# A pacing constant for weight conversions: STEP2 from 2800 to 1900 in an attention and gated-FFN kernel

## The chip, the cores and the metric

The kernel runs on one core of one Trainium2 chip. The metric is the device time of one execution in microseconds (us). The core's engines are named as in the profile: PE does the matrix products and PEld loads their weights, DVE is the vector engine, ACT the scalar engine, POOL the general engine, and SP issues nearly all DMAs, in the order of its own queue. Each engine works its instructions off in a fixed order, which is settled when the kernel is built.

## The reference

Block-causal attention over 8 batches of 8 heads (576 positions, head size 64), and behind it a bilinear feed-forward layer over all 4608 tokens (512 to 1536 to 512), in float32:

```python
scores = scale * np.matmul(q, k.transpose(0, 1, 3, 2))
scores = np.where(mask, scores, -1000000000.0)          # by blocks of 64
attn = np.exp(scores - max); attn = attn / (sum + 1e-09)
x = (attn @ v).transpose(0, 2, 1, 3).reshape(B * S, H * D)
a = x @ w_a
b = x @ w_b
out = (a * b) @ w_out
```

The weights come in as 64-bit floats and are turned into float32 on the chip.

## The kernel before, in words

The hidden size of 1536 is 12 blocks of 128 ("f" 0 to 11), done in three passes of four blocks. A product in float32 is made of three products of rounded parts (high by high, low by high, high by low), so each operand is held as a high and a low part. The first pass runs beside the attention. The second and third pass each go over 6 pairs of token tiles of 384 (`tt`, 768 tokens each, here called a tile pair), and what follows is about these two passes alone.

For one tile pair and one f the function `pair_unit` (a unit) makes the products by a scheme with 7 products of 6 matmuls in place of 8: four into four PSUM banks y, x, w, v, and then a second one on top of x, w and v. Between them DVE must read the banks: L729 reads x (and a copy of y by ACT) and must be done before the second product on x, L731 reads w before the second on w, L733 reads v before the second on v. L735 to L739 make the two hidden tiles, ACT (L110) rounds each to its high part, and POOL (L113) makes its low part. After four units `pair_out` multiplies with W_out: 96 matmuls into 8 banks (L757), each of which DVE adds to a partial sum that SP loaded (L816), and SP stores the sum (L817).

Beside this, DVE and ACT prepare the next tile pair's x: SP loads four tiles of it (L665), `sums_x` forms differences (L675, L676, L679, L682) and low parts (L689 to L692).

The weights are converted by a generator, `convert_w`, that is advanced step by step. A part of W_a and W_b (two for each f) takes 6 steps: L139, L143, L145, L147 and L149 on DVE take the 64-bit numbers apart and build float32, L172 (four small ones) forms sums, L177 and L178 the low parts. A part of W_out (one for each f) takes 5 steps: L139 to L149 and one L113 on DVE. The parts for the third pass are converted during the second: each is loaded by SP (L124), written to memory when it is done (L205), and read back when the third pass's buffers come free (L842 for W_a and W_b, during the last tile pair, L857 for W_out, behind it). They are 8 x 6 + 4 x 5 = 68 steps in all.

How fast the generator is advanced is set by `background`: `k` counts matmuls of the units (4 x 42 = 168 for a tile pair), and after each one the generator is brought up to `start + k * T2 / 2.4 / pace` steps. From the end of the second pass's first tile pair on, `pace` is STEP2. What is left behind the last tile pair is done there in one go:

```python
if ps_ == 0 and tt == 0:
    background(1e4)
    conv = convert_w(parts(range(F1 + F2, NF)), nc.vector, paced=True, stage=stage)
    n_conv, start, k, pace = 0, 0, 0, STEP2
pair_out(fs, hs, nm, out)
if ps_ == 0 and tt == NT2 - 1:
    background(1e4)
```

A conversion's DVE instructions are bound to stand behind the latest L739 (`behind_of`, key "hf"). For the rest a scheduler in the kernel library settles each engine's order when the kernel is built, from the order of the code, its dependences and its own estimates of durations.

Of the kernel before, what the change touches and what calls it, by code (L numbers as in the profile page):

```python
# [38 lines left out]
MORE = 6  # L39
PREF = True  # L40
STEP = 800
STEP2 = 2800
LATE = 1
LO2 = lambda nc: nc.vector
CONVP = [1]*12
# [7 lines left out]
def attention_then_bilinear_ffn(  # L53
# [101 lines left out]
    def parts(fs):  # L155
        return [(f, i) for f in fs for i in range(KP)] + [(f, KP) for f in fs]
# [23 lines left out]
    def convert_w(todo, lo_eng, paced=False, stage=None):  # L180

        def ahead(f, i):
            return fetch(wab[f, :, i] if i < KP else wo[f], f"w{f}_{i}")

        raw = ahead(*todo[0])
        for k, (f, i) in enumerate(todo):
            now, raw = raw, ahead(*todo[k + 1]) if k + 1 < len(todo) else None
            xf, spare = yield from convert(now, f"w{f}_{i}", paced)
            if stage:
                st = stage.tile([P, 2, NW if i < KP else NO, P], F32R, tag="st", name=f"st{f}_{i}")  # L190
            if i == KP:
                if not stage and w_sb[f][1] is None:
                    new_wo(f)
                o = st.rearrange("p j c n -> p j (c n)") if stage else w_sb[f][1]
                split(o[:, 0], o[:, 1], xf, nc.scalar, lo_eng)
            elif f < F1:
                ab = w_sb[f][0]
                hi, lo = (ab[:, j, i].rearrange("p c n -> p (c n)") for j in range(2))
                split(hi, lo, xf, nc.scalar, lo_eng)
            else:  # L200
                ab = st if stage else w_sb[f][0][:, i]
                yield from sums(ab[:, 0], ab[:, 1], xf, spare, paced)
            if stage:
                f -= F1 + F2
                nc.sync.dma_start(wod[f] if i == KP else wabd[f, i], f32(st).rearrange("p j c n -> p (j c n)"))  # L205
            yield
# [536 lines left out]
    def pair_out(fs, hs, nm, out):  # L743

        todo = [(j, o) for j in (1, 0) for o in range(NO)]
        n = {}

        def run(j, o, fs_):
            k = j, o
            if k not in n:  # L750
                n[k] = 0, bank(f"pso{j}_{o}_{nm}")[:, :T2]
            i, ps = n[k]
            osl = slice(o * P, (o + 1) * P)
            for f in fs_:
                (hh, hl), wt = hs[f][j], w_sb[f][1]
                for a, b in ((0, hh), (0, hl), (1, hh)):
                    nc.tensor.matmul(ps, wt[:, a, osl], b, start=i == 0, stop=i == 3 * len(fs) - 1)  # L757
                    i += 1
            n[k] = i, ps
            if i == 3 * len(fs):  # L760
                out(j, o, ps)

        for k in todo[:2]:
            run(*k, fs[:-1])
        for k in todo[:2]:
            run(*k, fs[-1:])
        for k in todo[2:]:
            run(*k, fs)
# [34 lines left out]
    for ps_ in range(2):  # L803
        fs = list(range(F1 + ps_ * F2, F1 + (ps_ + 1) * F2))
        for tt in range(NT2):
# [42 lines left out]
# [5 lines that stand above are left out]
# [44 lines left out]
```

## Time and profile before

| | |
|---|---|
| time, three runs | 1268.36, 1269.23, 1271.0 us; median 1269.23 |
| the profiled execution | 1273.54 us, of which its span (first to last instruction) is 1271.6 |
| busy share of the span | PE 97%, PEld 92%, DVE 79%, ACT 54%, POOL 44% |
| second pass, units and products | about 697 to 983 us from the span's start |
| third pass | about 983 us to the end |
| DVE busy, 742 to 960 us | 189.30 of 218.00 us (87%) |
| DVE busy, 1000 to 1272 us | 173.84 of 272.00 us (64%) |
| PE busy, 960 to 1000 us | 35.45 of 40.00 us |

Times inside the execution are us from the span's start. In a timeline a row is: start, duration, engine, line, operation, tile written from tiles read, count, and in brackets the idle time of the engine before it and what ended it; short idle times have no bracket. In a table of stretches the columns are: the stretch, its length, busy time and count of PE, PEld, DVE, ACT and POOL, the clock that PE was granted (1.00 is full), the share of the DMA engines that was busy, and GB/s. A matmul's duration in the rows overlaps the next one's: 6 matmuls of 384 columns take 1.06 us.

### The profile page before, as it was taken

Reading aid. Unit: us, or ns where it says so; the run is one execution under the profiler, and the core shown is the slowest. Engines: PE = TensorE matmul, PEld = TensorE weight load, DVE = VectorE, ACT = ScalarE, POOL = GpSimd, SP = SyncE. Lnnn points to the kernel's source line nnn. Section 1 sums busy time; section 2 is a strip of 40 time slices with the busy share of each in tenths; the row PEclk is TensorE's granted clock in tenths of the full one; section 3 lists DMA queues with packets and bytes.
Section 4 is the critical chain, followed back from the end, with each engine's and each line's share of the span. In section 5 each row is a group of like instructions: output and inputs, shape, how many; then the busy total and the mean of one; then the engine's idle time right before and its main releaser. Section 6 shows DMA issues by size and latency. Waiting matters only on the chain.

```text
span 1271.6 us, 23516 instructions
## 1 busy us (share of the span) xinstructions
PE 1235.8 (97%) x7849; PEld 1172.4 (92%) x7849; DVE 1006.1 (79%) x2389; ACT 683.3 (54%) x1722; POOL 556.9 (44%) x679
## 2 busy tenths in 40 slices
PE   9988999999999999999998999999999999999998
PEld 5668999999999999999998999999999899999998
DVE  6979877777887777877799999899879877577553
ACT  5788787878887788777745423323313322122210
POOL 4667566556565565665423223222222223123231
PEclk8999999999999999999998999999999899999999
DMA  5557767777667767676225264364287752243131
GB/s 197 147 162 198 193 166 182 184 169 180 173 164 185 170 175 174 164 179 162 88 95 161 96 195 132 109 195 155 86 286 260 240 149 83 67 149 103 48 100 62
DMA packets 93496, 196.58 MB, mean 155 GB/s; under 512 B 11968, under 2 KB 52928, under 8 KB 93376
## 3 DMA queue, kind: packets, MB, share of 16 engines
q1 hardware_dynamic: 88768, 185.64, 51.8%
q10 hardware_dynamic: 4608, 9.44, 2.0%
q8 instruction: 63, 1.03, 0.3%
q14 instruction: 57, 0.47, 0.1%
HBM read 96.47 MB, written 47.19 MB: 113 GB/s over the span
## 4 chain that ended last, share of the span: by engine, by line
PE 74%; DVE 14%; issue 3%; DMA 3%; ACT 3%; POOL 2%; SPq 0%; ACTq 0%; DVEq 0%; POOLq 0%
PE pso_z L757 14%; PE ps L217 12%; PE tp L468 7%; PE psx_z L711 7%; PE psw_z L711 6%; PE pso L217 5%; PE psv_z L711 5%; PE s L392 4%; PE av L517 3%; PE psy_z L711 3%; PE av L523 3%; PE sl L392 2%; DMA kp<-kT 2%; DVE sw L147 1%; DVE nm L398 1%
## 5 line engine op out<-in xcount | busy, mean ns | idle before, releaser
L113 POOL TENSOR_TENSOR h_z<-u_z,h_z 128x384 fp32r<-128x384 f32 x96 | 111.0, 1157 | 395.4 <-ACT h_z L110 370.2
L217 PE MATMUL ps<-xh,wab 128*128 128x288 f32 x1024 | 241.4, 303 | 1.2 <-ACT a L241 1.2
L445 POOL TENSOR_SCALAR e<-e,rc 128x512 f32<-128x512 f32 (+3 forms) x256 | 153.1, 610 | 125.3 <-DVE rc L442 118.6
L757 PE MATMUL pso_z<-h_z,wo 128*128 128x384 f32 x1152 | 203.4, 335 | 1.2 <-POOL h_z L113 1.2
L757 PEld LDWEIGHTS pso_z<-h_z,wo 128*128 128x128 f32 x1152 | 199.7, 188 | 2.6 <-POOL h_z L113 2.6
L217 PEld LDWEIGHTS ps<-xh,wab 128*128 128x128 f32 x1024 | 171.9, 188 | 4.7 <-ACT a L241 1.4
L472 DVE TENSOR_TENSOR al<-tp,ah 128x512 fp32r<-128x512 f32 x224 | 131.5, 608 | 34.0 <-ACT ah L470 33.8
L217 PE MATMUL ps<-xl,wab 128*128 128x288 f32 x512 | 153.9, 301 | 0.0
L468 PE MATMUL tp<-ident,e 128*128 128x128 f32 x832 | 135.8, 278 | 11.1 <-POOL e L445 4.0
L470 ACT CAST ah<-tp 128x512 fp32r<-128x512 f32 x224 | 116.6, 533 | 50.8 <-PE tp L468 47.9
L110 ACT CAST h_z<-u_z 128x384 fp32r<-128x384 f32 x96 | 49.4, 514 | 164.4 <-DVE u_z L736 157.3
L217 PE MATMUL pso<-hh,wo 128*128 128x288 f32 x512 | 128.1, 311 | 4.4 <-ACT hh L110 4.4
L468 PEld LDWEIGHTS tp<-ident,e 128*128 128x128 f32 x832 | 100.4, 141 | 26.8 <-POOL e L445 10.4
L711 PE MATMUL psx_z<-xh,wab 128*128 128x384 f32 x384 | 118.2, 344 | 4.3 <-DVE u_z L729 3.6
L401 ACT ACTIVATE e<-s,nm 128x192 f32<-128x192 f32 (+2 forms) x192 | 101.7, 530 | 32.0 <-DVE nm L398 23.0
L711 PE MATMUL psw_z<-xh,wab 128*128 128x384 f32 x384 | 117.1, 341 | 1.3 <-DVE u_z L731 1.3
L711 PE MATMUL psv_z<-xh,wab 128*128 128x384 f32 x384 | 117.0, 339 | 0.0
L398 DVE TENSOR_REDUCE nm<-s 128x1 f32<-128x192 f32 (+3 forms) x256 | 109.9, 431 | 2.4
L217 PEld LDWEIGHTS ps<-xl,wab 128*128 128x128 f32 x512 | 96.4, 188 | 3.4
L217 PEld LDWEIGHTS pso<-hh,wo 128*128 128x128 f32 x512 | 88.4, 192 | 6.6 <-ACT hh L110 5.3
L113 POOL TENSOR_TENSOR v<-vr,v 128x320 fp32r<-128x320 f32 x56 | 50.4, 899 | 87.8 <-ACT v L110 71.3
L392 PE MATMUL s<-k,q 128*128 128x256 f32 x336 | 81.3, 322 | 3.1 <-ACT e L401 1.5
(142 smaller groups left out, 2926.3 us busy)
## 6 DMA issues: line engine op xcount, KB each, us to landing
k<-kp SPq DMA_DIRECT2D x112, 288.0 KB, 3.6
xr<-xd SPq DMA_DIRECT2D x48, 384.0 KB, 3.4
pt<-part SPq DMA_DIRECT2D x96, 192.0 KB, 3.5
q<-qp SPq DMA_DIRECT2D x112, 160.0 KB, 2.6
raww<-wab SPq DMA_DIRECT2D x24, 512.0 KB, 3.8
qp<-qT SPq DMA_DIRECT2D x32, 320.0 KB, 3.2
vr<-vm SPq DMA_DIRECT2D x64, 160.0 KB, 3.2
kp<-kT SPq DMA_DIRECT2D x32, 288.0 KB, 3.5
```

The costliest lines, as they stand in the source:

```text
L110: nc.scalar.copy(hi, src)
L113: return lo_eng.tensor_tensor(lo, src, f32(hi), op=ALU.subtract)
L217: mm = nc.tensor.matmul(ps, w_, d_, start=(i == 0), stop=(i == n - 1))
L392: mark = nc.tensor.matmul(ps[:, :w], qm[:, q0[t]:q0[t] + P], kk[:, :w], start=(i == 0), stop=(i == len(ks) - 1))
L398: nc.vector.tensor_reduce(nm[:, t:t + 1], view, axis=AX.X, op=ALU.max, negate=True)
L401: nc.scalar.activation(out, view, AF.Exp, bias=bias, accum_out=sm[:, t, :1])
L445: nc.gpsimd.tensor_scalar(ev, ev, rc[:, t:t + 1], 1.0, op0=ALU.mult, op1=ALU.mult)
L468: mark = nc.tensor.transpose(tp[:, c], src, ident)
L470: nc.scalar.copy(ah[:, :m, cols], tp[:, :m])
L472: return nc.vector.tensor_tensor(al[:, :m, cols], tp[:, :m], f32(ah[:, :m, cols]), op=ALU.subtract)
L711: nc.tensor.matmul(ps, wt[:, i, iw], j[:, ix], start=start and kp == 0 and i == 0 and j is xh, stop=kp == KP - 1 and i == 1, skip_group_ch ...
L757: nc.tensor.matmul(ps, wt[:, a, osl], b, start=i == 0, stop=i == 3 * len(fs) - 1)
```

## The change

One constant:

```diff
 STEP = 800
-STEP2 = 2800
+STEP2 = 1900
 LATE = 1
```

For a tile pair of 168 matmuls the generator is now advanced by 168 x 160 / 1900 = 14.1 steps in place of 168 x 160 / 2800 = 9.6. In the five tile pairs behind the first this comes to 70.7 in place of 48, so all 68 steps are made before the last `pair_out`, where 20 were left for the place behind it (all four parts of W_out). No instruction's work is changed: the same conversions stand in other places, and with them their DMAs.

In the rows that follow, `u_z_1_5` is the unit of tile pair 1 and f = 5, and `u_z_0_8` the first unit of the third pass; a row is a line, an operation, the tile written and the tiles read, and its size.

DVE in tile pair 1 of the second pass, between the units of f = 4 and f = 5, before:

```order
L739 TENSOR_TENSOR u_z_1_4_11090<-psx_z_1_4_11049,u_z_1_4_11090 128x384
L147 SCALAR_TENSOR_TENSOR sw_0_11057<-raww_0_11053,sw_0_11057 128x512
L149 TENSOR_TENSOR xw_0_11059<-mw_0_11058,sw_0_11057 128x512
L729 TENSOR_TENSOR u_z_1_5_11165<-psx_z_1_5_11133,u_z_1_5_11165 128x384
L172 TENSOR_TENSOR mw_0_11058<-xw_0_11059 128x128 x2
L172 TENSOR_TENSOR mw_0_11058<-mw_0_11058,xw_0_11059 128x128
L731 TENSOR_TENSOR u_z_1_5_11166<-psw_z_1_5_11134,u_z_1_5_11165 128x384
```

The same place now:

```order
L739 TENSOR_TENSOR u_z_1_4_11091<-psx_z_1_4_11049,u_z_1_4_11091 128x384
L149 TENSOR_TENSOR xw_0_11059<-mw_0_11058,sw_0_11057 128x512
L172 TENSOR_TENSOR mw_0_11058<-xw_0_11059 128x128 x2
L172 TENSOR_TENSOR mw_0_11058<-mw_0_11058,xw_0_11059 128x128
L177 TENSOR_TENSOR st_0_11144<-xw_0_11059,st_0_11144 128x384
L172 TENSOR_TENSOR mw_0_11058<-xw_0_11059,mw_0_11058 128x128
L729 TENSOR_TENSOR u_z_1_5_11176<-psx_z_1_5_11134,u_z_1_5_11176 128x384
L139 TENSOR_SCALAR sw_1_11189<-raww_1_11055 128x512
L178 TENSOR_TENSOR st_0_11144<-mw_0_11058,st_0_11144 128x512
L731 TENSOR_TENSOR u_z_1_5_11177<-psw_z_1_5_11135,u_z_1_5_11176 128x384
```

Six conversion instructions stand between the two units' work in place of two, and between L729 and L731 two large ones in place of three small ones.

DVE at the change of passes, ahead of the first L729 of the third pass, before (`raww_2` and `st_2` belong to parts of W_out, `xr_1` and `xt_1` to the x of the third pass's second tile pair):

```order
L149 TENSOR_TENSOR xw_2_13404<-mw_2_13403,sw_2_13402 128x512
L675 TENSOR_TENSOR xt_1_0_13682<-xr_1_13533,xr_1_13531 128x384
L139 TENSOR_SCALAR sw_2_13417<-raww_2_13400 128x512
L113 TENSOR_TENSOR st_2_13411<-xw_2_13404,st_2_13411 128x512
L816 TENSOR_TENSOR pt_3_5_0_13308<-pso_3_z_5_13385,pt_3_5_0_13308 128x384
L143 TENSOR_SCALAR mw_2_13418<-raww_2_13400 128x512
L147 SCALAR_TENSOR_TENSOR sw_2_13417<-raww_2_13400,sw_2_13417 128x512
L145 SCALAR_TENSOR_TENSOR mw_2_13418<-raww_2_13400,mw_2_13418 128x512
L676 TENSOR_TENSOR xr_1_13531<-xr_1_13531 128x384
L149 TENSOR_TENSOR xw_2_13419<-mw_2_13418,sw_2_13417 128x512
L729 TENSOR_TENSOR u_z_0_8_13498<-psx_z_0_8_13467,u_z_0_8_13498 128x384
```

The same place now:

```order
L675 TENSOR_TENSOR xt_1_0_13682<-xr_1_13533,xr_1_13531 128x384
L676 TENSOR_TENSOR xr_1_13531<-xr_1_13531 128x384
L816 TENSOR_TENSOR pt_1_5_0_13155<-pso_1_z_5_13413,pt_1_5_0_13155 128x384
L679 TENSOR_TENSOR xt_1_0_13682<-xr_1_13533,xr_1_13531 128x384
L682 TENSOR_TENSOR xt_1_0_13682<-xr_1_13533,xt_1_0_13682 128x384
L816 TENSOR_TENSOR pt_2_5_0_13359<-pso_2_z_5_13428,pt_2_5_0_13359 128x384
L816 TENSOR_TENSOR pt_3_5_0_13366<-pso_3_z_5_13443,pt_3_5_0_13366 128x384
L675 TENSOR_TENSOR xt_1_1_13762<-xr_1_13537,xr_1_13535 128x384
L676 TENSOR_TENSOR xr_1_13535<-xr_1_13535 128x384
L679 TENSOR_TENSOR xt_1_1_13762<-xr_1_13537,xr_1_13535 128x384
L682 TENSOR_TENSOR xt_1_1_13762<-xr_1_13537,xt_1_1_13762 128x384
L729 TENSOR_TENSOR u_z_0_8_13498<-psx_z_0_8_13467,u_z_0_8_13498 128x384
```

The conversions are gone from there, and all eight instructions on the next tile pair's x, which read all four loads `xr_1`, now stand ahead of L729; before, six of them came behind it.

SP's queue at the same place now, where those loads are issued:

```order
L665 DMA xr_1_13533<-xd 128x768
L812 DMA pt_3_5_0_13366<-part_58 128x384
L817 DMA part_59<-pt_2_5_0_13149 128x384
L817 DMA part_59<-pt_3_5_0_13151 128x384
L817 DMA part_59<-pt_0_5_0_13153 128x384
L665 DMA xr_1_13535<-xd 128x768
L817 DMA part_59<-pt_1_5_0_13155 128x384
L665 DMA xr_1_13537<-xd 128x768
```

The loads' places are nearly those of before (there `pt_1_5` was stored ahead of the third load, and three DMAs of the conversions stood between the third and the fourth). The fourth load is queued behind the store of `pt_1_5`, whose L816 now stands on DVE behind the first two instructions on `xr_1`.

## The prediction

> **What bounds the kernel now.** I read the table of stretches first, cut from one block of W_out products to the next, so that each row is one tile pair: three of the second pass, then its last one together with the first of the third pass, then two undisturbed ones of the third pass.
>
> ```profile
> 775.84:823.07 47.23, 47.01 (x265) 45.87 (x265) 42.77 (x71) 14.99 (x27) 13.27 (x10) 1.00 0.45 151
> 823.07:870.61 47.54, 47.21 (x265) 45.97 (x265) 43.01 (x71) 14.27 (x26) 12.95 (x10) 1.00 0.45 142
> 870.61:918.10 47.49, 47.15 (x266) 45.97 (x265) 41.25 (x65) 13.96 (x25) 13.27 (x10) 1.00 0.46 150
> 918.10:1019.16 101.06, 96.47 (x530) 94.86 (x529) 85.67 (x144) 30.99 (x54) 26.87 (x20) 0.97 0.72 247
> 1019.16:1065.64 46.48, 46.48 (x266) 46.32 (x265) 31.36 (x51) 11.38 (x21) 13.18 (x10) 1.00 0.34 103
> 1065.64:1112.09 46.45, 46.45 (x265) 46.28 (x265) 31.36 (x51) 11.38 (x21) 13.18 (x10) 1.00 0.33 102
> ```
>
> PE is busy throughout, and a tile pair on which nothing is converted takes 46.45 us. So PE's own work is the floor, and all that the change can move is what stands above it: 0.78, 1.09 and 1.04 us in tile pairs 2 to 4, and 101.06 - 2 x 46.45 = 8.2 us in the double stretch. With some 0.9 for tile pair 1 (an estimate after the other three) that is **12 us** in all. PE's longer waits and the clock show where the 8.2 went:
>
> ```profile
> 963.75 0.44 PE L711 MATMUL psx_z<-xh,wab 128*128 128x384 f32 x1 [1.15 <-DVE u_z L729]
> ...
> 969.85 0.62 PE L757 MATMUL pso_z<-h_z,wo 128*128 128x384 f32 x2 [0.41 <-POOL h_z L113]
> ```
>
> ```profile
> 989.82 0.44 PE L711 MATMUL psx_z<-xh,wab 128*128 128x384 f32 x1 [1.73 <-DVE u_z L729]
> 992.38 0.69 PE L711 MATMUL psw_z<-xh,wab 128*128 128x384 f32 x1 [1.25 <-DVE u_z L731]
> ```
>
> ```profile
> 990.00:1000.00 10.00, 8.75 (x34) 8.43 (x35) 8.05 (x17) 3.69 (x6) 1.41 (x1) 0.66 0.87 285
> ```
>
> About 2.1 belong to tile pair 5 (1.15 and 0.41, some 0.3 each for restarting and for an earlier short wait). The other **6.1 are the change of passes**: 1.73 and 1.25 of waiting, and about 3 of a clock granted at 0.66 over the ten us behind it. DVE's own rows there say whose work was in the way:
>
> ```profile
> 988.14 0.55 DVE L676 TENSOR_TENSOR xr<-xr 128x384 f32<-128x384 f32 x1
> 988.61 0.68 DVE L149 TENSOR_TENSOR xw<-mw,sw 128x512 f32<-128x512 f32 x1
> 989.21 0.55 DVE L729 TENSOR_TENSOR u_z<-psx_z,u_z 128x384 f32<-128x384 f32 x1
> 991.10 0.43 DVE L139 TENSOR_SCALAR sw<-raww 128x512 int32<-128x512 int32 x1 [1.34 <-DMA raww<-wo]
> ...
> 991.78 0.55 DVE L731 TENSOR_TENSOR u_z<-psw_z,u_z 128x384 f32<-128x384 f32 x1
> ```
>
> L729 is late behind conversions without a gap, and L731 behind a conversion that waits for its own load. Both go with the change. What comes in their place decides the sign.
>
> **What the change removes.** The 20 steps at the change of passes, and so the 6.1 us, if nothing else is late there. In tile pair 5 the last unit loses its conversions too.
>
> **What it adds in tile pairs 1 to 5.** The same DVE work, nearer together. The unit of DVE time that matters is the place between L739 and the next L729, where conversions are bound to stand. The view of DVE and of POOL at such a place of tile pair 3, which holds L149 and three of L172:
>
> ```profile
> 848.24 1.28 DVE L149 TENSOR_TENSOR xw<-mw,sw 128x512 f32<-128x512 f32 x1
> 849.55 1.20 DVE L172 TENSOR_TENSOR mw<-xw 128x128 f32<-128x128 f32 x2
> 850.67 0.28 DVE L172 TENSOR_TENSOR mw<-mw,xw 128x128 f32<-128x128 f32 x1
> 850.88 0.54 DVE L729 TENSOR_TENSOR u_z<-psx_z,u_z 128x384 f32<-128x384 f32 x1
> 851.35 0.28 DVE L172 TENSOR_TENSOR mw<-xw,mw 128x128 f32<-128x128 f32 x1
> 851.54 0.55 DVE L177 TENSOR_TENSOR st<-xw,st 128x384 fp32r<-128x384 f32 x1
> 852.01 0.55 DVE L731 TENSOR_TENSOR u_z<-psw_z,u_z 128x384 f32<-128x384 f32 x1
> ```
>
> ```profile
> 847.94 1.03 POOL L113 TENSOR_TENSOR h_z<-u_z,h_z 128x384 fp32r<-128x384 f32 x1 [17.00 <-ACT h_z L110]
> 849.31 1.09 POOL L113 TENSOR_TENSOR h_z<-u_z,h_z 128x384 fp32r<-128x384 f32 x1 [0.34 <-PE psx_z L711]
> ```
>
> Two of its DVE instructions each last until just after one of POOL's two L113 (848.97 and 850.40), which adds about 1.3 us whatever stands there. By the same conversions without POOL, at the change of passes, the rest is cheap:
>
> ```profile
> L113 DVE TENSOR_TENSOR st<-xw,st 128x512 fp32r<-128x512 f32 x4 | 2.8, 691 | 0.6 <-ACT st L110 0.6
> L147 DVE SCALAR_TENSOR_TENSOR sw<-raww,sw 128x512 int32<-128x512 int32 x4 | 2.8, 688 | 0.0
> ...
> L143 DVE TENSOR_SCALAR mw<-raww 128x512 int32<-128x512 int32 x4 | 1.7, 419 | 0.0
> ```
>
> Tile pairs 2 to 4 have three such places each, all of two or three large instructions or of this kind, for 0.78 to 1.09 us: **0.33 for a place**. So this length is just beyond what PE's first products cover, and each further instruction is paid at its distance from the next one's start: 0.6 for a large one, 0.35 for L139 or L143, 0.47 for L177 and 0.2 for an L172. [...] Were instead every conversion at such a place slowed as L149 is, by 0.6, the three long places below would be 1.2 dearer each, and the sum 3.6 higher.)
>
> The order of the changed kernel gives, unit by unit:
> - three long places (tile pairs 1, 2, 4) that end with L177 and the fourth L172 ahead of L729: 0.33 + 0.47 + 0.2 = 1.0, and behind L729 an L139 and an L178 ahead of L731: 1.0 where 0.66 (L172 and L177, above) just fitted, 0.3. Together 1.3 each;
> - three places with L143, L147 and L145, in tile pairs 2, 4 and 5: one more 0.47 than the usual, 0.8 each;
> - six usual places and two of L139 and L143, 0.33 each;
> - in tile pair 3 L177 and L172 ahead of an L731 (0.5), and three more pairs of L139 with L178 or L113 ahead of an L731 or L733, 0.3 each;
> - one L147 more at the end of tile pair 1. There DVE has no slack:
>
> ```profile
> 795.98 0.55 DVE L729 TENSOR_TENSOR u_z<-psx_z,u_z 128x384 f32<-128x384 f32 x1
> ```
>
> ```profile
> 796.58 0.44 PE L711 MATMUL psx_z<-xh,wab 128*128 128x384 f32 x1
> ```
>
> so another 0.6. The sum is 3.9 + 2.4 + 2.6 + 0.5 + 0.9 + 0.6 = 10.9, and with 0.3 for the next pair's L675 and L676 in tile pair 5 it is 11.2, against 0.9 + 2.9 + 2.1 = 5.9 before: **5.3 us more**. I would not trust it to better than 2.
>
> **What comes at the change of passes instead.** The unit's L729 now stands behind all eight instructions on `xr_1`, the last four of which need its third and fourth load. The rows for these loads (SP's issues, ACT's first reader, and the medians to landing of the two earlier, the two later, and the four of the third pass's first tile pair):
>
> ```profile
> 978.51 0.48 SPq L665 DMA_DIRECT2D xr<-xd  x1
> ...
> 989.09 0.92 SPq L665 DMA_DIRECT2D xr<-xd  x1
> ```
>
> ```profile
> 983.93 0.84 ACT L683 CAST xh<-xr 128x768 fp32r<-128x768 f32 x1 [1.53 <-DMA xr<-xd]
> ```
>
> ```profile
> xr<-xd SPq DMA_DIRECT2D x2, 384.0 KB, 4.5
> ```
>
> ```profile
> xr<-xd SPq DMA_DIRECT2D x2, 384.0 KB, 5.8
> ```
>
> ```profile
> xr<-xd SPq DMA_DIRECT2D x4, 384.0 KB, 3.4
> ```
>
> On the clock of before: nothing ahead of the second load is changed, so it is issued at 978.5 and there at 983.9. DVE, free since about 981.3, then does L675, L676 and the L816 of `pt_1_5` (3 x 0.5); SP stores that and only then issues the fourth load, at about 985.7. With 4.5 us to land it is there at 990.2; four instructions (1.9) and L729 (0.55) end at 992.7. PE ran dry at 989.82 - 1.73 = 988.1 before; ten W_out products that ran ahead in the stalls of tile pair 5 now come behind it, so it wants L729 at about 988.7. **PE waits 4.0 us**, and by 3.4 to 5.8 us of landing 2.9 to 5.3; if the second load too lands in 3.4, 2 less. The transfers of `raww` and `wod` that shared this stretch are gone, so I take 4.5 and not 5.8. Nothing else can run in the wait: in the changed order PE's next row is the second product on x of that unit.
>
> The clock: 1.73 and 1.25 idle within 4.3 us cost it half its rate for some 7 us. Less did not:
>
> ```profile
> 960.00:970.00 10.00, 8.44 (x47) 7.80 (x46) 8.87 (x18) 4.77 (x8) 2.29 (x3) 1.00 0.67 253
> ```
>
> 4.0 idle in one piece is more than either, so I count the same 3 us again. The change of passes then costs 4.0 + 0.1 + 3 = 7.1 in place of 6.1. **Sum**: +5.3 + 1.0 = +6.3. The profiled execution took 1273.54 us (2 around its span of 1271.6), 4.3 above the median of 1269.23; the same difference put on the median gives **1275.5 us**.
>
> **The rivals.**
> - *The wait without the clock's drop*: 3 less, 1272.5. [...] 0.18.
> - *The loads come in time*: if the fourth lands before about 986 on this clock, L729 is ready by 988.7 and the change of passes is free: 5.3 - 6.1 = -0.8, 1268.4. It would need the second load by 982 and the fourth in 2.5. 0.13.
> - *Faster*: the loads come in time, and the added steps in the tile pairs cost no more than those of before, 1.0 x 14.1 / 9.6 = 1.5 for each of five, 7.3 in place of 5.9: +1.4 - 6.1 = -4.7, **1264.5**. It is decided by the same landing at 986, and by the long places costing 0.5 and not 1.0. 0.09.
> - *The clock drops in the tile pairs too*: a long place puts 1.0 and 0.2 of idle within 2 us. Each drop would cost 3: 1278 to 1285. Tile pair 5 had 1.15 and 0.41 at a clock of 1.00 (above). 0.08.
>
> That the change might not do what it says is no rival: the order shows no conversion behind the last L816 of the second pass.
>
> **How the numbers follow.** The forecast has 0.52 and, by the landing, 1272 to 1279 as its own range. About 0.2% (2.5 us) is what a measurement of this kernel can tell from no change. Faster by more: the third rival and a little of the second, 0.10. Within it: most of the second, half of the first, 0.22. Slower: the rest, 0.68. The range of 1267.5 to 1280 leaves out the third rival, the low end of the second and most of the fourth.
>
> **What would show it.** Tile pairs 1 to 4 at 48 to 49.5 us from one block of W_out to the next, and the waits for L729 of 0.7 to 0.9 at the three long places; L675 on `xr_1` with an idle time of DVE that a load ends, twice; the first second product on x of the third pass behind a wait of 3 to 5 us, and a clock under 0.8 there. It would be wrong if the double stretch of tile pair 5 and the next is under 96 us, or if tile pairs 1 to 4 stay at 47.5.

## The result, and the profile after

| | before | changed |
|---|---|---|
| median of six runs | 1268.83 us | 1278.23 us |
| lowest to highest | 1263.68 to 1271.34 | 1277.07 to 1280.99 |
| the profiled execution, its span | 1273.54, 1271.6 | 1277.07, 1275.3 |

The ratio is 1.0062, with a 95% interval of 1.0041 to 1.0083: **slower, by some 7.9 us** by the ratio (the two medians differ by 9.4), where +6.3 was forecast. The median of 1278.23 us lies inside the stated range, 2.7 above the forecast of 1275.5.

The tables of stretches below are cut from the last W_out product of one tile pair to the last of the next: tile pairs 1 to 5 of the second pass, and as the sixth row the first tile pair of the third pass with the change of passes ahead of it. The columns are those of the prediction's tables. Before:

```profile
745.17:792.14 46.97, 46.67 (x265) 45.78 (x265) 41.66 (x68) 13.69 (x26) 13.22 (x10) 1.00 0.44 137
792.14:839.37 47.23, 47.01 (x265) 45.87 (x265) 42.77 (x69) 14.65 (x25) 12.98 (x10) 1.00 0.47 153
839.37:886.92 47.55, 47.22 (x265) 45.98 (x265) 42.98 (x72) 15.61 (x27) 13.26 (x10) 1.00 0.48 158
886.92:934.41 47.49, 47.15 (x266) 45.97 (x266) 40.56 (x65) 12.09 (x22) 13.26 (x10) 1.00 0.44 139
934.41:983.15 48.74, 47.13 (x265) 46.17 (x265) 40.17 (x67) 13.11 (x23) 13.24 (x10) 1.00 0.78 277
983.15:1035.63 52.48, 49.49 (x266) 48.69 (x266) 46.34 (x80) 19.03 (x31) 13.77 (x10) 0.93 0.67 218
```

The changed kernel:

```profile
742.52:791.08 48.56, 47.32 (x266) 45.93 (x265) 44.96 (x78) 16.07 (x29) 13.35 (x10) 1.00 0.49 153
791.08:840.55 49.47, 47.32 (x265) 45.67 (x265) 46.00 (x78) 16.31 (x28) 12.94 (x10) 1.00 0.53 181
840.55:889.23 48.68, 47.42 (x266) 45.88 (x266) 44.68 (x74) 14.56 (x27) 13.18 (x10) 1.00 0.49 162
889.23:937.92 48.69, 47.34 (x265) 45.76 (x265) 43.37 (x70) 14.70 (x26) 13.37 (x10) 1.00 0.50 162
937.92:985.71 47.79, 47.22 (x265) 45.91 (x265) 39.66 (x60) 13.64 (x23) 12.94 (x10) 1.00 0.76 264
985.71:1039.20 53.49, 47.93 (x265) 47.45 (x265) 35.41 (x59) 13.46 (x23) 13.14 (x10) 0.94 0.45 144
```

Row by row the change costs 1.59, 2.24, 1.13, 1.20, then -0.95, and +1.01 in the last: **5.2 us in tile pairs 1 to 5 and 1.0 at the change of passes, 6.2 in all.** In the last row DVE does 11 us less work than before (35.41 against 46.34) and PE still needs 1 us more: the work is gone and another wait stands in its place. PE's rows with the longer waits show both kinds:

```profile
755.30 0.44 PE L711 MATMUL psx_z<-xh,wab 128*128 128x384 f32 x1 [0.77 <-DVE u_z L729]
796.10 0.44 PE L711 MATMUL psx_z<-xh,wab 128*128 128x384 f32 x1 [0.44 <-DVE u_z L729]
803.92 0.44 PE L711 MATMUL psx_z<-xh,wab 128*128 128x384 f32 x1 [0.27 <-DVE u_z L729]
812.34 0.44 PE L711 MATMUL psx_z<-xh,wab 128*128 128x384 f32 x1 [0.72 <-DVE u_z L729]
820.79 0.45 PE L711 MATMUL psx_z<-xh,wab 128*128 128x384 f32 x1 [0.72 <-DVE u_z L729]
860.99 0.44 PE L711 MATMUL psx_z<-xh,wab 128*128 128x384 f32 x1 [0.63 <-DVE u_z L729]
870.53 0.44 PE L711 MATMUL psw_z<-xh,wab 128*128 128x384 f32 x1 [0.42 <-DVE u_z L731]
902.00 0.44 PE L711 MATMUL psx_z<-xh,wab 128*128 128x384 f32 x1 [0.78 <-DVE u_z L729]
910.05 0.44 PE L711 MATMUL psx_z<-xh,wab 128*128 128x384 f32 x1 [0.31 <-DVE u_z L729]
958.45 0.45 PE L711 MATMUL psx_z<-xh,wab 128*128 128x384 f32 x1 [0.38 <-DVE u_z L729]
995.85 0.69 PE L711 MATMUL psx_z<-xh,wab 128*128 128x384 f32 x1 [5.56 <-DVE u_z L729]
```

Each of the waits in the tile pairs costs its idle time and about 0.26 more until PE's matmuls keep step again: at 755.30 the matmul starts 1.11 us behind the one before it and the next 0.28 behind that, where 0.177 each is the rule. The three long places are those at 755.30, 812.34 and 902.00. The last row is the first second product on x of the third pass, 0.69 us long where the others take 0.44 or 0.45, at half the clock (0.50 granted from 992.27 to 999.10):

```profile
990.00:1000.00 10.00, 4.44 (x17) 4.15 (x16) 4.10 (x8) 0.00 (x0) 0.00 (x0) 0.66 0.98 358
```

Before, the same ten us had 0.66 too, with 34 matmuls where there are 17 now.

DVE's rows ahead of that wait, SP's issues, and the time to landing of the last of them:

```profile
984.88 0.56 DVE L675 TENSOR_TENSOR xt<-xr,xr 128x384 f32<-128x384 f32 x1 [2.05 <-DMA xr<-xd]
985.47 0.56 DVE L676 TENSOR_TENSOR xr<-xr 128x384 f32<-128x384 f32 x1
985.95 0.55 DVE L816 TENSOR_TENSOR pt<-pso_z,pt 128x384 f32<-128x384 f32 x1
...
992.99 0.56 DVE L675 TENSOR_TENSOR xt<-xr,xr 128x384 f32<-128x384 f32 x1 [4.50 <-DMA xr<-xd]
...
995.25 0.55 DVE L729 TENSOR_TENSOR u_z<-psx_z,u_z 128x384 f32<-128x384 f32 x1
```

```profile
986.53 0.32 SPq L817 DMA_DIRECT2D part<-pt  x1
986.95 0.37 SPq L665 DMA_DIRECT2D xr<-xd  x1
```

```profile
xr<-xd SPq DMA_DIRECT2D x1, 384.0 KB, 5.9
```

The chain of the prediction can be read off: L816 (985.95) ends, SP stores its tile (986.53), only then issues the fourth load (986.95). That takes 5.9 us to land, and DVE stands with L729 behind it.

### The profile page after: what moved, and what is told of

Same layout as the page of the kernel before. It is cut to its first block, busy times and chain, and to the rows that moved or that the text cites. A ratio compares the mean times of both kernels' runs of the same rounds, so it can differ in the third digit from the quotient of the medians.

```text
span 1275.3 us, 23521 instructions
## 1 busy us (share of the span) xinstructions
PE 1235.5 (97%) x7849; PEld 1170.6 (92%) x7849; DVE 1005.7 (79%) x2389; ACT 683.0 (54%) x1722; POOL 554.7 (43%) x679
## 3 DMA queue, kind: packets, MB, share of 16 engines
q8 instruction: 63, 1.03, 0.3%
## 4 chain that ended last, share of the span: by engine, by line
PE 69%; DVE 17%; DMA 4%; issue 4%; ACT 3%; POOL 2%; SPq 0%; ACTq 0%; DVEq 0%; POOLq 0%
PE pso_z L757 13%; PE ps L217 12%; PE tp L468 7%; PE psx_z L711 6%; PE psw_z L711 6%; PE pso L217 5%; PE psv_z L711 5%; PE s L392 4%; PE av L517 3%; PE av L523 3%; PE psy_z L711 2%; PE sl L392 2%; DMA kp<-kT 2%; DVE nm L398 1%; DVE sw L147 1%
## 5 line engine op out<-in xcount | busy, mean ns | idle before, releaser
L113 POOL TENSOR_TENSOR h_z<-u_z,h_z 128x384 fp32r<-128x384 f32 x96 | 109.9, 1146 | 402.8 <-ACT h_z L110 385.7
L757 PE MATMUL pso_z<-h_z,wo 128*128 128x384 f32 x1152 | 203.1, 335 | 0.7 <-POOL h_z L113 0.7
L757 PEld LDWEIGHTS pso_z<-h_z,wo 128*128 128x128 f32 x1152 | 199.9, 188 | 1.9 <-POOL h_z L113 1.9
L113 POOL TENSOR_TENSOR v<-vr,v 128x320 fp32r<-128x320 f32 x56 | 50.2, 896 | 88.8 <-ACT v L110 63.5
L711 PEld LDWEIGHTS psx_z<-xh,wab 128*128 128x128 f32 x384 | 71.5, 189 | 17.5 <-DVE u_z L729 17.5
```

Of the source, the lines that this page charges most:

```text
L113: return lo_eng.tensor_tensor(lo, src, f32(hi), op=ALU.subtract)
L711: nc.tensor.matmul(ps, wt[:, i, iw], j[:, ix], start=start and kp == 0 and i == 0 and j is xh, stop=kp == KP - 1 and i == 1, skip_group_ch ...
```

## The experiments

The stretches are cut as above. Where an edit adds two lines to the kernel, the line numbers behind them are two higher in its rows (L731 is L729 then, L735 is L733, L741 is L739, L759 is L757, L818 is L816, L691 to L694 are L689 to L692).

| stretch, us | tile pair 1 | 2 | 3 | 4 | 5 | first of pass 3 | sum |
|---|---|---|---|---|---|---|---|
| before | 46.97 | 47.23 | 47.55 | 47.49 | 48.74 | 52.48 | 290.5 |
| before, again | 46.99 | 47.23 | 47.49 | 47.44 | 48.73 | 51.15 | 289.0 |
| changed | 48.56 | 49.47 | 48.68 | 48.69 | 47.79 | 53.49 | 296.7 |
| changed, again | 48.54 | 50.07 | 48.64 | 48.73 | 47.83 | 54.70 | 298.5 |
| x behind the first unit | 48.53 | 49.94 | 48.64 | 48.65 | 47.83 | 46.47 | 290.1 |
| loads issued by ACT | 48.55 | 49.58 | 48.67 | 48.73 | 47.83 | 46.34 | 289.7 |
| conversions behind L733 | 46.42 | 53.29 | 46.32 | 46.66 | 46.32 | 54.04 | 293.1 |
| capped at 48 steps | 48.51 | 49.81 | 48.67 | 47.03 | 46.49 | 51.89 | 292.4 |
| both edits, 1900 | 46.39 | 53.63 | 46.32 | 46.64 | 46.32 | 46.47 | 285.8 |
| both edits, 2000 | 46.86 | 46.46 | 52.81 | 46.32 | 46.63 | 47.83 | 286.9 |
| both edits, 2200 | 46.32 | 46.32 | 46.32 | 46.32 | 46.92 | 47.40 | 279.6 |
| both edits, 2800 | 46.51 | 46.32 | 46.32 | 46.47 | 46.72 | 48.52 | 280.9 |

### Do the two profiles repeat?

The kernel before and the changed one, each profiled once more.

> The kernel before, unchanged, profiled a second time. The first profile has the second pass from 697.0 us and, from the last W_out product of its first tile pair to that of the third pass's first, 290.5 us. Theory (the stages from the second pass on repeat, and it is the first pass that differs from run to run): these stages at 290 to 291 again, each tile pair within 0.3, the start of the second pass anywhere from 691 to 700. Rival (the second pass itself differs from run to run, and the profile shown was a bad one): the stages 2 or more under 290.5.

> The changed kernel, unchanged, profiled a second time. The first profile has the second pass from 694.3 us and the same stages at 296.7 us, with a wait of 5.6 us for the third pass's first L729. Theory: stages at 296 to 297.5 again, the wait at 5 to 6, the start of the second pass anywhere from 692 to 700. Rival (the landing of the fourth load is chance): the wait falls to under 4 or rises over 7, with the stages by as much.

The tile pairs repeat within 0.1 us, but for tile pair 2 of the changed kernel (0.6, in the wait at 796.10, which was 1.04 the second time). The change of passes doesn't: 51.15 against 52.48, and 54.70 against 53.49. Neither theory had that: the waits are nearly the same (1.75 and 0.89 the second time before, 5.33 in the changed kernel), but the half clock covers other work. In the changed kernel's first profile it lasted from 992.27 to 999.10, so 3.3 us of it fell on work behind the wait; in the second from 997.90 to 1004.73, and 5.9 did. The second profile's row:

```profile
988.91:1043.61 54.70, 49.37 (x266) 48.88 (x265) 35.30 (x59) 13.45 (x23) 13.13 (x10) 0.94 0.43 145
```

By the two pairs of profiles these stages cost +6.2 and +9.5; the runs say +7.9.

### Is the wait at the change of passes DVE's order alone?

The first edit binds the third pass's second x behind the last L739 of that pass's first unit:

```diff
             if nm == f"0_{NT2}":
                 behind_of(ins, "hf")
+            if nm == "1_1":
+                behind_of(ins, "first")
...
                     background(start + k * T2 / 2.4 / pace)
+                if i == 0 and ps_ == 1 and tt == 0:
+                    last["first"] = last["hf"]
```

> The change, with one dependence more: the eight DVE instructions (first two of each half, the rest follow them) on the x of the third pass's second tile pair may only stand behind the last L739 of the third pass's first unit, not ahead of its first L729. Conversions stand where the change has them. Theory: the wait of 5.6 us for that L729 and the half clock behind it are only DVE's queue standing behind the late fourth load, so both go: 7 us less than the changed kernel, 1271 us (1269.5 to 1272.5), ratio to the kernel before 1.000 to 1.003; the granted clock is 1.00 from 985 on, and the double stretch of tile pair 5 and the next takes 94 to 95 us; tile pairs 2 to 4 stay at 48.7 to 49.2. Rival A, a wait takes its place (the x is late for the next tile pair, or L731 and L733 of the second unit stand behind the loads): 1274 to 1278. Rival B, most of the change's cost is in the tile pairs, and the wait was mostly paid before too: 1274 or more, with the clock unchanged.

The stretch of the change of passes falls from 53.49 to 46.47, which is the floor, and the clock is full:

```profile
941.68:989.52 47.84, 47.19 (x266) 45.93 (x266) 39.96 (x60) 13.63 (x23) 12.97 (x10) 1.00 0.76 264
989.52:1035.98 46.46, 46.46 (x265) 46.29 (x265) 35.51 (x58) 13.55 (x23) 13.54 (x10) 1.00 0.50 165
```

So all of the 7 us was DVE's queue standing behind a load that nothing needed yet. The total is 1273.59 us, a ratio of 1.0028 (1.0011 to 1.0045), 1.1 us above the range that I had given. The stages came out as said, but for tile pair 2 (49.94, where 49.2 was the top). The second pass began at 697.6 us in this profile and at 694.3 in the changed kernel's; more on this start below.

The second edit leaves DVE's instructions free and lets ACT issue the same four loads:

```diff
+    third = [False]
...
-            nc.sync.dma_start(
+            (nc.scalar if tt == 1 and third[0] else nc.sync).dma_start(
...
+                    third[0] = ps_ == 1
                     raw = load_x((tt + 1) % NT2)
```

> The change, with the four loads of the x of the third pass's second tile pair issued by ACT's queue in place of SP's, so that the fourth is no longer behind the store of the tile that DVE adds behind its first two instructions on that x. Theory: the fourth load is late because SP issues it late (986.95 us) and shares the rings with what SP issued around it; issued by 982 to 984 it lands by 988, the wait for the first L729 falls from 5.6 to between 0 and 1.5 us, with no half clock, and the time to 1271 to 1273.5. Rival: it is the transfers themselves (5.9 us under the third pass's other loads) that are late, whoever issues them: the wait stays above 3 us, 1276 or more; or the issues of ACT delay its own copies, which the waits would show as PE waiting for ACT.

1270.94 us, ratio 1.0004 (0.9994 to 1.0014), so no difference to the kernel before can be told, and the stretch is 46.34. ACT's last issue, DVE's first reader of the fourth load, and PE's first second product on x:

```profile
982.66 0.39 ACTq L667 DMA_DIRECT2D xr<-xd  x1
```

```profile
988.27 0.56 DVE L677 TENSOR_TENSOR xt<-xr,xr 128x384 f32<-128x384 f32 x1 [1.28 <-DMA xr<-xd]
```

```profile
991.94 0.44 PE L713 MATMUL psx_z<-xh,wab 128*128 128x384 f32 x1
```

It is still some 5.5 us from the issue until DVE can start (982.66 to 988.2), but the issue comes 4.3 us earlier, though the second pass of this profile began 1.5 us later, and L729 (L731 here) is done before PE asks for it: no wait, with all eight instructions on that x still ahead of it on DVE. It is SP's order that was late; the transfer was slow in both (5.5 and 5.9 us, where the median for the third pass's first tile pair in the kernel before was 3.4), and that it was slow by what SP issued around it is not shown.

### Is it the place of the conversions that costs in the tile pairs, or DVE's load?

The third edit binds conversions behind the latest L733 in place of L739, so that they fall where DVE waits for PE's second products:

```diff
-                behind_of(ins, "hf")
+                behind_of(ins, "cv" if "cv" in last else "hf")
...
-            behind_of(ins, "hf")
+            behind_of(ins, "cv" if "cv" in last else "hf")
...
-        v.tensor_tensor(t, v_, t, op=ALU.add)
+        last["cv"] = v.tensor_tensor(t, v_, t, op=ALU.add)
```

> The change, with the conversions bound behind the last L733 in place of the last L739, so that they stand mostly between L733 and L735, where DVE waits for PE's second products, and not between L739 and the next unit's L729. The change of passes is as in the changed kernel. Theory: what the change pays in the tile pairs (about 2.3 us each above the floor of 46.45, in place of 1.0) is the length of DVE's row ahead of the next L729, so most of it goes: tile pairs 2 to 4 at 46.6 to 47.5 us, 5 to 8 us less in all, 1270 to 1273 with the wait of 5 to 6 us at the change of passes still there. Rival: DVE's load as a whole is what costs (it is over 90% busy there), and the late L735 to L739 delay the second products of the next unit or POOL's low parts: tile pairs stay at 48 to 49.5, 1276 to 1282.

Four of the five tile pairs fall to 46.3 to 46.7 us, the floor or close to it, with the same number of steps, tile pair 1 with DVE at 43.7 of 46.4 us busy. So DVE had room for 14 steps a tile pair; it was the place that cost. But the total is 1276.88, ratio 1.0051 (1.0039 to 1.0064), above what I expected: tile pair 2 took 53.29, with PE waiting 4.64 us for POOL's L113 ahead of the W_out products. Neither theory had that. It comes back, of the same length, in the next run.

> The two edits together: conversions behind L733, and the x of the third pass's second tile pair behind the third pass's first unit. Theory: both costs are of DVE's order alone and add: 7 us less by the change of passes and 5 to 8 less by the tile pairs, 1263 to 1266, under the kernel before by 0.2 to 0.5%. Rival: the half of it, 1268 to 1271, if only one of the two holds; 1272 or more if neither.

1267.77 us, ratio 0.9987 (0.9976 to 0.9997): both costs are off, but the new one is there, and so the time is above the 1263 to 1266 of the theory. The rows of PE, POOL and DVE there:

```profile
831.01 1.33 PE L759 MATMUL pso_z<-h_z,wo 128*128 128x384 f32 x3 [4.64 <-POOL h_z L113]
```

```profile
825.17 6.76 POOL L113 TENSOR_TENSOR h_z<-u_z,h_z 128x384 fp32r<-128x384 f32 x2 [6.32 <-ACT h_z L110]
```

```profile
824.14 0.68 DVE L178 TENSOR_TENSOR st<-mw,st 128x512 fp32r<-128x512 f32 x1
824.74 0.55 DVE L741 TENSOR_TENSOR u_z<-psx_z,u_z 128x384 f32<-128x384 f32 x1
825.21 0.95 DVE L691 TENSOR_TENSOR xl<-xr,xh 128x768 fp32r<-128x768 f32 x1
...
829.15 0.95 DVE L692 TENSOR_TENSOR xl<-xt,xh 128x768 fp32r<-128x768 f32 x1
832.05 0.56 DVE L818 TENSOR_TENSOR pt<-pso_z,pt 128x384 f32<-128x384 f32 x1 [1.95 <-PE pso_z L759]
```

POOL's two L113, of 1.02 to 1.22 us each in most other units of these tile pairs, took 6.76, the first of them 5.78: from L691 at 825.21 to the end of L692 at 830.1 six instructions of DVE went ahead of it, and PE goes on at 831.01, one L113 later. DVE's rows have no gap from 820.41 to 830.1. My reading was that the run of conversions L149 to L178 in the tile pair's last unit had closed the gap ahead of the next x's low parts. If that is so, the wait has to move with that run. With STEP2 at 2000 it stands in the last unit of tile pair 3, with 2200 in none:

```diff
-STEP2 = 1900
+STEP2 = 2000
```

> The two edits together with STEP2 at 2000. Here the run L149, L172 to L178 in a last unit stands in tile pair 3 and not in tile pair 2. Theory: the wait of PE for POOL's L113 of 4 to 5 us, with half clock behind it, moves to tile pair 3, which takes 52.5 to 54 us, and tile pair 2 takes 46.3 to 46.8. Rival (something of tile pair 2 itself, such as its loads): the wait stays in tile pair 2 or is gone.

> The two edits together (conversions behind L733, the x of the third pass's second tile pair behind the third pass's first unit) with STEP2 at 2200. With 1900 these two took 53.6 us for tile pair 2, 7.3 over the others: PE waited 4.64 us for POOL's L113, which took 6.76 us for two because DVE's rows left no gap between a long run of conversions (L149 to L178) in the tile pair's last unit and L691 to L694. With 2200 no last unit holds that run. Theory (DVE without a gap keeps POOL out): every tile pair at 46.3 to 46.8 us, no wait over 1 us for L113 from 750 us on, 7 us under the version with 1900, so 1259 to 1262, a ratio of 0.992 to 0.995 to the kernel before. Rival (the wait comes from the rate of conversions behind L733 as such, or ACT's rounding): a wait of 2 us or more for L113 comes back in some tile pair, 1264 to 1269.

At 2000 (one execution, 1272.94 us) the wait is in tile pair 3, of the same size, and tile pair 2 is at 46.46:

```profile
879.18 1.27 PE L759 MATMUL pso_z<-h_z,wo 128*128 128x384 f32 x4 [4.64 <-POOL h_z L113]
```

```profile
873.34 6.76 POOL L113 TENSOR_TENSOR h_z<-u_z,h_z 128x384 fp32r<-128x384 f32 x2 [6.32 <-ACT h_z L110]
```

At 2200 it is gone; POOL, DVE at the same place, and the stretches:

```profile
824.02 1.03 POOL L113 TENSOR_TENSOR h_z<-u_z,h_z 128x384 fp32r<-128x384 f32 x1 [5.63 <-ACT h_z L110]
825.45 1.30 POOL L113 TENSOR_TENSOR h_z<-u_z,h_z 128x384 fp32r<-128x384 f32 x1 [0.40 <-POOL h_z L113]
```

```profile
823.63 0.56 DVE L741 TENSOR_TENSOR u_z<-psx_z,u_z 128x384 f32<-128x384 f32 x1
824.10 1.76 DVE L691 TENSOR_TENSOR xl<-xr,xh 128x768 fp32r<-128x768 f32 x1
825.79 1.78 DVE L692 TENSOR_TENSOR xl<-xt,xh 128x768 fp32r<-128x768 f32 x1
```

```profile
792.37:838.69 46.32, 46.32 (x265) 46.32 (x265) 41.84 (x73) 14.85 (x26) 13.30 (x10) 1.00 0.54 174
...
931.33:978.25 46.92, 46.77 (x265) 46.23 (x265) 40.64 (x69) 14.86 (x25) 12.64 (x10) 1.00 0.81 276
978.25:1025.65 47.40, 46.89 (x265) 46.17 (x265) 37.50 (x61) 14.92 (x25) 13.17 (x10) 1.00 0.54 182
```

So the wait goes with that run of conversions: all three profiles that have the run in a last unit have the wait. But the missing gap is not the reason. At 2200 DVE's rows have no gap ahead of L691 either (824.10 begins 0.47 behind L741, as 825.21 does at 1900), and POOL's L113 are through in 1.03 and 1.30 all the same, beside L691 and L692, which take 1.76 and 1.78 in place of 0.95. Nor is it decided by which of the two starts first. In the three late cases L113 begins 0.04 us ahead of L691. At 2200 it begins 0.08 ahead, in tile pair 1 at 2000 0.03 ahead (779.55), and in tile pair 1 at 1900 0.42 behind, and each time it is through behind one instruction of DVE at most. What in the run of conversions lengthens the L113 to 5.78 stays open.

This version, **both edits with 2200, beats both kernels**: 1263.66 us against 1271.20 of the kernel before beside it, ratio 0.9945 (0.9929 to 0.9962). It is still above the 1259 to 1262 of the theory; tile pair 5 took 46.92, just over its 46.8.

### What is the constant worth then?

> The two edits together with STEP2 at 2800, the constant of the kernel before, so that 20 steps are left again for the change of passes. Theory: tile pairs 1 to 4 at 46.3 to 46.8 as with the other constants, 3.4 us less than the kernel before; tile pair 5 and the change of passes as before, 52 to 53.5 for the block-to-block stretch of the first tile pair of the third pass, since the conversions stand there as before: 1264.5 to 1267.5. So with the conversions behind L733 a change of STEP2 to 2200 is worth 4 to 7 us, where in the kernel as it was it was a loss. Rival (the conversions at the change of passes cost little once they may stand behind L733): 1259 to 1262, no difference to 2200.

1266.34 us, ratio 0.9963 (0.9946 to 0.998). The tile pairs are at the floor as said, and the change of passes is far below what I expected (48.52; 20 steps are left there, but behind L733 they held PE up by 1.34 us at most, with the clock at 1.00). So the rival was nearer in the stages: 280.9 against 279.6. That the time fell into the theory's range is chance, as the stage that it rested on was over 3 us off. What the constant is worth there is 1.3 us by the stages and 2.7 by the medians; the intervals of 2200 and 2800 overlap, so the size is not settled.

### Does a step cost the same wherever it stands?

```diff
-                    background(start + k * T2 / 2.4 / pace)
+                    background(min(start + k * T2 / 2.4 / pace, F2 * PER_F if pace == STEP2 else 1e9))
```

> The change, with the steps capped at the 48 of W_a and W_b until the last W_out products of the second pass: tile pairs 1 to 3 and the first unit of 4 are as in the changed kernel, the rest of 4 and 5 hold no conversion, and the 20 steps of W_out stand at the change of passes as in the kernel before. Theory (the cost is that of the places that hold conversions): by the stretches from one block's last product to the next one's, tile pairs 1 to 3 take 48.6, 49.5 and 48.7 as in the changed kernel (5.0 more than before in sum), tile pair 4 47.2 to 47.6, tile pair 5 46.5 to 47.5 (1.5 less than before), the change of passes 52 to 54: +2.5 to +4.5 on the kernel before in these stages, 1272 to 1274.5. Rival (each step costs the same wherever it stands): no difference to the kernel before, 1268 to 1271.

1277.24 us, ratio 1.004 (1.0024 to 1.0055), +5.1 us on the 1271.20 beside it and above the expected 1274.5; by the stages +1.9 and +3.4 on the two profiles of before. Steps were only packed into fewer tile pairs, and the three packed ones cost 5.2 us more than before and the two emptied ones 2.7 less. So a step has no price of its own, as the theory said. PE's wait at the change of passes:

```profile
989.99 0.69 PE L711 MATMUL psx_z<-xh,wab 128*128 128x384 f32 x1 [2.71 <-DVE u_z L729]
```

Behind this one wait of 2.71 the clock stood at half (0.69 for the matmul; 0.93 granted over the whole stretch).

## Why the prediction was right, and where its sizes were off

The time (1275.5, range to 1280) and the mechanism held: nothing is won at the change of passes, because a wait for the fourth load takes the place of the wait for conversions, and the tile pairs pay for the steps.

**What the change removes.** Right. With the new wait taken out as well, the stretch is 46.3 to 46.5, 4.7 to 6.1 us under the two profiles of before.

**Tile pairs 1 to 5.** Forecast +5.3, measured +5.2 and +5.9; above five times the floor of 46.45 they stand at 10.9 in the first profile, where 11.2 was forecast. The terms inside it were less good, and it is partly luck that their errors cancel. From the starts of PE's matmuls in the changed kernel's first profile, with the 0.26 of restarting:
- The three long places, priced at 1.3, took 1.21, 1.14 and 1.21. Of the 0.3 in it for L139 and L178 ahead of L731, 0.17 came.
- The three places with L143, L147 and L145, priced alike at 0.8, took 0.99 (820.79), 0.44 (918.18) and 0.65 (958.45).
- The eight places at 0.33 took 0.36 to 0.57, and one of them 0.90 (860.99).
- The extra L147 of tile pair 1, 0.6, took 0.71, and 1.31 in the second profile.

The place at 860.99 holds two small instructions:

```profile
858.35 0.95 DVE L139 TENSOR_SCALAR sw<-raww 128x512 int32<-128x512 int32 x1
859.22 1.24 DVE L143 TENSOR_SCALAR mw<-raww 128x512 int32<-128x512 int32 x1
```

```profile
858.00 2.19 POOL L113 TENSOR_TENSOR h_z<-u_z,h_z 128x384 fp32r<-128x384 f32 x2 [6.42 <-ACT h_z L110]
```

Both last until behind one L113 each, 1.35 together over the 0.42 that each takes alone. So the fixed price of POOL (1.3) held at this place too. That what it costs PE depends on when POOL starts, which I had not put into the price, fits these rows, but no run moved POOL alone.

**The change of passes.** 7.1 above the floor was forecast, 7.0 and 8.2 were measured. That the first profile came so near is luck, as two errors offset each other there. The wait was 5.56 (5.33 in the second), not 4.0: the fourth load took 5.9 us to land (4.5 taken, up to 5.8 in the bounds), and from its landing to the end of L729 it was 2.9 us, not 2.5. The clock cost 1.6 us in the first profile and 3.0 in the second (half of 3.3 and 5.9 us), where 3 was taken: part of the half clock falls into the wait itself, where it costs nothing. What slowed that fourth load stays open. The W_out loads that SP issued behind it, at 987.42 and from 989.57 on, are not needed for it: with the loads issued by ACT, SP issued the first of them at 991.44, and the fourth load still took some 5.5 us.

**The median.** Put on the median, the difference of 6.3 was 1.6 too small by the ratio and 3.1 by the medians. The two pairs of profiles alone span +6.2 to +9.5 in these stages, for the most part by where the half clock falls. Besides, the second pass began between 694.2 and 700.1 us in the profiled executions. In the kernel before and the changed one the order ahead of it is the same on each engine, and it began at 697.0 and 697.6 before, at 694.3 and 696.8 in the changed kernel. These few us of the first pass are in every total, and what sets them stays open. The version with 2200, 9 to 11 us faster by its stages, began its second pass about 1 us later than before, at 698.5. That is a part of why it is only 7.5 faster by its runs; the rest is not shown.

**The rivals.** The wait without the clock's drop is out (0.66 granted from 990 to 1000, as before), and loads in time could be had, but only by another queue or order. With them goes the faster one, which rested on the same landing. The clock did not drop in the tile pairs: it was 1.00 in all five.

## What to carry to other kernels

Work that is spread into another engine's slack was priced here by its place in the row, not by its amount: the same steps cost 5 us ahead of an instruction that PE waits for, and close to nothing in the gap behind the last one it waits for (tile pairs of 46.3 to 46.7 us against the floor of 46.45), as long as no third engine pays for them. When work is moved away from a place, look at what the scheduler pulls into it, above all instructions that wait for a load, and at what that load is queued behind. And a row that costs one neighbour nothing any more can hold up another: here POOL, once, for 4.64 us of PE's time. Look at every engine that waits, in the rows, before a new order is called free.

## What the runs showed of the hardware that was not expected

- One L113 on POOL took 5.78 us in place of 1.03, beside six instructions of DVE without a gap, in three runs (1900 with conversions behind L733, alone and with both edits, and 2000). In other last units POOL's and DVE's instructions went on side by side, also with no gap in DVE's row: at 2200 the L113 took 1.03 and 1.30, and L691 and L692 1.76 and 1.78 in place of 0.95. What decides between the two no run shows.
- The half clock came with one idle gap of PE of 2.71 us (steps capped at 48, 0.93 granted over the stretch), and not with gaps of 1.34 (2800, 1.00 over the stretch) and 0.98 (2000). It began 1.9 us into that gap, 2.0 and 4.4 into those of 5.56 and 5.33, and at 2000 only 0.5 us behind the end of the gap of 4.64. The half clock lasted 6.83 us in most cases, and 3.41 us in that case at 2000 and in the second profile of before.
